# DeltaNet and a maxout layer on one core: the opening's chain rebuilt, and identity products put into TensorE's waits

## The chip, the cores and the metric

One core of one Trainium2 chip. The metric is the time of one execution in microseconds (us), the median of three runs. The engines are named as the profile names them: PE (matrix products; PEld its weight loads), DVE (VectorE), ACT (ScalarE), POOL (GpSimd), SP (SyncE, which here only issues DMAs). Each works through its own instructions in order and waits on semaphores for the others.

## The reference

Attention of the delta-rule kind, then a feed-forward layer with the maximum of three products:

```python
B, H, S, D = 4, 8, 768, 48
k_n = k / (np.linalg.norm(k, axis=-1, keepdims=True) + 1e-06)
state = np.zeros((B, H, D, D))
for t in range(S):
    kt, vt, bt = k_n[:, :, t], v[:, :, t], beta[:, :, t, None]
    y[:, :, t] = einsum('bhd,bhde->bhe', q[:, :, t], state)
    v_old = einsum('bhde,bhd->bhe', state, kt)
    state = state + bt[..., None] * einsum('bhd,bhe->bhde', kt, vt - v_old)
x = y as (3072 tokens, 384)
h = max(x @ w1, x @ w2, x @ w3)      # 384 x 768 each
out = h @ w_out                      # 768 x 384
```

## The kernel before, in words

The recurrence is cut into 12 chunks of 64 positions. In each chunk the 64 updates depend on one another through a triangular system, one for each of the 32 (batch, head) pairs, made of the products of the keys among themselves, scaled by beta over the squared norms. The kernel inverts the 32x32 diagonal blocks of these systems by elimination on DVE (`solve`), for two chunks at a time, 128 blocks side by side on the partitions, and joins the blocks by small products on PE. With the inverse, the updates of a chunk are products, and the state is carried from chunk to chunk. Queries, keys and values come from DRAM; a token's outputs are turned (`to_x`) and go into the feed-forward layer, which runs over six groups of 512 tokens.

The order of all instructions is written out by hand, engine by engine (a manual schedule): the order of the Python calls is the order of each engine's queue. Nothing reorders it.

The opening is what comes before the first feed-forward product, the calls from `busy(6, ident)` to the loop over `ffn(0)`. Its steps, with the names that later text uses:

- `turn(n, (0,))` and `turn(n, (1,))` transpose the keys or queries of unit n on PE (a unit is one chunk of two of the four batches); ACT, once DVE, copies the result from PSUM (L335). `kpad`, `kmore` and `qall` are the loaded keys and queries.
- `keys(n)` and `gram(n, (1,))` are the key-by-key and query-by-key products (`p_g`, L406) with a copy from PSUM to `at` (L423) or `pt` (L417). For the units 4 to 7 the blocks go by DMA to DRAM (`to_dram`, L436, on SP) and come back block by block (`blocks(1)`, L483, issued on POOL).
- For the units 0 to 3 `to_blocks` (L467, L465) copies the blocks from `at` and `first_blocks` (L471) transposes them all in one DVE instruction.
- `solve(0)` computes the norms (`norm`, L261 to L266: a root on ACT and five small DVE instructions that refine it), the inverse, its square times beta (L523 to L525), writes the diagonal (L529), scales (L538), and runs 15 steps of two DVE instructions (L552, L556). It then transposes the solution (L564) and `placed` (L496) copies it, block by block, into `ut`. `solve(1)` does the same for the next two chunks in 31 steps, a few after each feed-forward group.
- `halves_t` (L633, L635) transposes the solution for the left side of a product. `halves_z` (`p_e`, L673) and `halves_u` (`p_f`, L684, L688) join 16x16 halves to 32x32 blocks, `turn_t1` (L618, L620), `join_z` (`p_z`, L701, L705) and `join_u` (`p_j`, L714, L716) join 32x32 blocks to 64x64.
- `new(0)` (`p_u`, L759, L764) gives the updates, `to_y(0)` (`p_y`, L801, L805) the outputs, `to_x(0)` (`p_x`, L820, L827) turns them. `masked` (L390) applies the triangle to `pt`. `scale` (L287) multiplies the values by the norms, which `first_norms` (L302) has transposed on DVE.

The weights arrive as 64-bit numbers. `fetch` loads one of 24 pieces (L215, on SP or POOL); one step of `conv` turns a piece into 32-bit numbers with three ACT instructions (L238 to L240), and `joined` (L250 on DVE, L254 on POOL) puts the halves of the piece before together.

PSUM is handed out in two rings: `two`, three buffers of two banks, and `ffn`, two buffers of one bank. A product waits until the buffer's earlier reader is done. `busy(n, of)` runs n products of the identity with itself into an `ffn` buffer that nobody reads; one such product is two passes of 128x128 over 128 columns. Before the change it is called once, at the start.

After the opening, `ffn(0)` yields after each group of products (`hidden`, L1161, L1169, L1175), and the loop puts the other work between the groups: `FIRST` lists the links of the first chunks (`e1`, `f1`, `z1`, `j1` are the joins of chunk 1, `s0` the state's step, `S1` one step of the solve, `M2` and `M3` masks of query products, `P4` the product itself with its mask), and `CONVERTED` the groups after which a weight piece is converted.

Of the kernel before, what the change touches and what calls it, by code (L numbers as in the profile page):

```python
# [16 lines left out]
C = 64  # L17
DP = 64
BL = 32
# [4 lines left out]
def kernel(  # L24
# [196 lines left out]
    def weights():  # L221
# [3 lines left out]
        waiting = None  # L225
        for dst, _, (a, b) in pieces:
# [14 lines left out]
            if waiting:  # L241
                joined(*waiting)
            waiting = dst, mant, mant_v, up_v
            yield
        joined(*waiting)
        yield

# [11 lines left out]
    def norm(out, ksum, root, t):  # L259

        nc.scalar.sqrt(root, ksum)  # L261
        nc.vector.tensor_scalar_max(t, root, 1e-30)
        nc.vector.reciprocal(t, t)
        nc.vector.tensor_tensor(out=t, in0=t, in1=ksum, op=ALU.mult)
        nc.vector.tensor_tensor(out=t, in0=t, in1=root, op=ALU.add)
        nc.vector.tensor_scalar(  # L266
            out=out, in0=t, scalar1=0.5, scalar2=1e-6, op0=ALU.mult, op1=ALU.add
        )

# [29 lines left out]
    bl_0 = []  # L299

    def first_norms():
        nc.vector.transpose(out=nrm_0.rearrange("p c g h -> p (c g h)"), in_=bl_0[0])  # L302
# [152 lines left out]
    def to_blocks(n, engines):  # L455


        cc, g = divmod(n, 2)
        for i, engine in enumerate(engines):
            bb, half = divmod(i, 2)  # L460
            r, x0 = block(bb, half), 16 * cc + 8 * g
            to = in_rows(in_wo(0))[r, x0 : x0 + H]
            of = ats[n][r, :, BL * half : BL * (half + 1)]
            if engine is nc.scalar:
                engine.copy(to, of)  # L465
            else:
                engine.tensor_copy(to, of)  # L467
# [21 lines left out]
    def placed(cc, i, copy=nc.vector.tensor_copy, xs_of=slice(0, 2 * H)):  # L489
# [6 lines left out]
        copy(to[:, xs_of], of[:, xs_of])  # L496

    def solve(m):
# [13 lines left out]
        bl = small("bl", BL)  # L512
        norm(bl, diagonal(x), small("root_bl", BL), small("nt_bl", BL))
# [3 lines left out]
        if m:  # L517
            norms_of(m, bl)
            nc.vector.reciprocal(bl, bl)
        else:  # L520
            bl_0.append(bl)
            bl = small("inv_bl", BL)
            nc.vector.reciprocal(bl, bl_0[0])  # L523
        nc.vector.tensor_tensor(out=bl, in0=bl, in1=bl, op=ALU.mult)
        nc.vector.tensor_tensor(out=bl, in0=bl, in1=beta_bl[:, m] if m else beta_0, op=ALU.mult)  # L525
# [12 lines left out]
        nc.vector.tensor_tensor(out=xb, in0=xb, in1=by, op=ALU.mult)  # L538
        yield
        for j in range(size - 1):  # L540
            a, b = j + 1, size - 1 - j
# [20 lines left out]
        if m == 0:  # L562
            back = in_rows(xs[0])
            nc.vector.transpose(out=back, in_=y.rearrange("p c i -> p i c"))  # L564
            yield
            for i in range(4):
                if i % 2:
                    n = H * (i == 3)
                    if n:
                        placed(0, i, nc.vector.tensor_copy, slice(0, n))  # L570
                    placed(0, i, nc.scalar.copy, slice(n, 2 * H))
                else:
                    placed(0, i, nc.vector.tensor_copy)
            return
# [52 lines left out]
    def halves_t(c, parts=(0, 1)):  # L627
        if c not in fine:
            fine[c] = [square("t") for g in range(2)]
        src = [ut[c % NU][:, g].rearrange("p h x -> p (h x)") for g in range(2)]  # L630
        dst = [t.rearrange("p h x -> p (h x)") for t in fine[c]]
        if 0 in parts:
            nc.vector.transpose(out=dst[0], in_=src[0])  # L633
# [30 lines left out]
    def halves_z(c):  # L664
        if c > 1:
            halves_t(c)
# [807 lines left out]
```

## Time and profile before

| | us |
|---|---|
| median of three runs | 513.03 |
| the runs | 512.97, 513.03, 517.85 |
| span of the profiled execution | 510.5 |
| what lies around the span, against the median | 2.5 |

The profiled execution's own time isn't listed apart from the runs; its span stands 2.5 us below the median, and that difference is used wherever spans and medians are compared.

| engine | busy us | share of the span |
|---|---|---|
| PE | 491.1 | 96% |
| PE weight loads | 333.1 | 65% |
| DVE | 349.9 | 69% |
| ACT | 168.7 | 33% |
| POOL | 192.7 | 38% |

The page cuts the span into 40 slices of 12.8 us, and gives for each the busy tenths of each engine and the clock that the throttle granted to PE (9 is 0.9 or more of full speed). Other views give the busy time of each engine in a chosen stretch, with the clock as a number, and the instructions in order of time: start, duration, engine, line, operation, what it writes and reads, shape, how many, and, in brackets, the idle time of the engine before it with what ended it. A matrix product with 32-bit operands counts as two passes, so 32 products show as x64; a transposition on PE is one pass.

### The profile page before, as it was taken

Reading aid. Unit: us, or ns where it says so; the run is one execution under the profiler, and the core shown is the slowest. Engines: PE = TensorE matmul, PEld = TensorE weight load, DVE = VectorE, ACT = ScalarE, POOL = GpSimd, SP = SyncE. Lnnn points to the kernel's source line nnn. Section 1 sums busy time; section 2 is a strip of 40 time slices with the busy share of each in tenths; the row PEclk is TensorE's granted clock in tenths of the full one; section 3 lists DMA queues with packets and bytes.
Section 4 is the critical chain, followed back from the end, with each engine's and each line's share of the span. In section 5 each row is a group of like instructions: output and inputs, shape, how many; then the busy total and the mean of one; then the engine's idle time right before and its main releaser. Section 6 shows DMA issues by size and latency. Waiting matters only on the chain.

```text
span 510.5 us, 18528 instructions
## 1 busy us (share of the span) xinstructions
PE 491.1 (96%) x8016; PEld 333.1 (65%) x8016; DVE 349.9 (69%) x801; ACT 168.7 (33%) x320; POOL 192.7 (38%) x317
## 2 busy tenths in 40 slices
PE   7778989999999999999999999999999999999996
PEld 6567778756565565665555565555655556998796
DVE  5897799969996430899563987635897455456752
ACT  5585664884422242210252101252101412113210
POOL 7434372783491926670575770503130000000000
PEclk9755999999999999999999999999999999999999
DMA  8938869764055925353675454923343202230001
GB/s 111 192 64 221 194 151 155 195 199 100 5 148 140 175 46 130 99 143 83 144 136 130 120 137 94 174 37 92 80 116 81 44 3 64 54 71 2 0 17 46
DMA packets 106304, 53.49 MB, mean 105 GB/s; under 512 B 89712, under 2 KB 99984, under 8 KB 106224
## 3 DMA queue, kind: packets, MB, share of 16 engines
q1 hardware_dynamic: 94352, 31.35, 30.4%
q0 software_dynamic: 9472, 20.37, 16.4%
q8 instruction: 63, 1.03, 0.9%
q10 hardware_dynamic: 2400, 0.59, 0.6%
q14 instruction: 17, 0.14, 0.1%
HBM read 39.17 MB, written 13.11 MB: 102 GB/s over the span
## 4 chain that ended last, share of the span: by engine, by line
PE 73%; DVE 14%; DMA 5%; ACT 4%; SPq 2%; issue 2%; POOL 0%; DVEq 0%; ACTq 0%; POOLq 0%
PE p_h L1161 26%; PE p_o L1199 13%; PE p_o L960 9%; PE p_e L1102 3%; DVE tmp L552 3%; PE p_g L406 3%; PE p_c L1102 2%; PE p_m L894 2%; PE p_u L759 2%; DMA kmore<-in_k_dram 2%; PE p_k L731 2%; PE p_y L801 2%; DVE y_bl L556 2%; PE p_s L782 2%; PE p_j L714 1%
## 5 line engine op out<-in xcount | busy, mean ns | idle before, releaser
L1161 PE MATMUL p_h<-xt,w_sb 128*128 128x512 f32 (+1 forms) x450 | 187.5, 558 | 0.7 <-ACT xt L827 0.6
L1161 PEld LDWEIGHTS p_h<-xt,w_sb 128*128 128x128 f32 x450 | 82.3, 193 | 68.7 <-issue 61.8
L1199 PE MATMUL p_o<-wo_sb,h 128*128 128x384 f32 x192 | 65.3, 490 | 0.0
L1175 DVE TENSOR_TENSOR h<-h,p_h 128x512 f32<-128x512 f32 (+1 forms) x42 | 25.4, 606 | 53.9 <-PE p_h L1161 52.8
L552 DVE TENSOR_TENSOR tmp<-x_bl,y_bl 128x31 f32<-128x31 f32 (+20 forms) x139 | 51.3, 369 | 4.1
L556 DVE TENSOR_TENSOR y_bl<-y_bl,tmp 128x31 f32<-128x31 f32 (+20 forms) x139 | 48.5, 349 | 4.8
L1199 PEld LDWEIGHTS p_o<-wo_sb,h 128*128 128x128 f32 x192 | 35.7, 190 | 23.2
L364 POOL DMA_DIRECT2D turned<-in_q_dram x72 | 39.1, 551 | 4.3 <-POOL turned L359 2.9
L1205 ACT COPY o_sb<-p_o 128x384 f32<-128x384 f32 x16 | 7.7, 479 | 85.8 <-PE p_o L1199 79.8
L1171 ACT ACTIVATE h<-p_h 128x512 f32<-128x512 f32 x24 | 14.3, 597 | 63.4 <-PE p_h L1161 60.5
L254 POOL TENSOR_TENSOR w_sb<-mant,up 128x384 int32<-128x384 int32 x18 | 19.1, 1059 | 39.3 <-DVE mant L250 39.2
L406 PEld LDWEIGHTS p_g<-kqt 48*64 48x64 f32 x1216 | 24.6, 142 | 9.0 <-issue 6.4
L406 PE MATMUL p_g<-kqt 48*64 48x64 f32 (+1 forms) x1216 | 27.8, 242 | 0.9 <-ACT kqt L335 0.8
L789 DVE TENSOR_TENSOR st<-st,p_s 48x768 f32<-48x768 f32 (+1 forms) x18 | 17.1, 949 | 15.4 <-PE p_s L782 15.2
L120 POOL DMA_DIRECT2D kpad<-in_k_dram x32 | 21.8, 690 | 14.1 <-issue 12.7
L1199 PE MATMUL p_o<-w_sb,xt 128*128 128x384 f32 x72 | 25.2, 486 | 0.0
L139 POOL DMA_DIRECT2D v_t<-in_v_dram x14 | 11.5, 829 | 35.5 <-PE p_u L759 35.5
L390 DVE TENSOR_TENSOR pt<-p_g,mask 128x512 f32<-128x512 f32 x20 | 13.8, 688 | 15.9 <-PE p_g L406 15.8
L287 POOL TENSOR_TENSOR v_t<-v_t,nrm 128x768 f32<-128x768 f32 x12 | 17.9, 1493 | 9.0 <-DVE nrm L281 8.9
L359 POOL MEMSET turned<- 128x96 f32 x18 | 3.3, 192 | 47.6 <-DVE kqt L380 47.6
L759 PEld LDWEIGHTS p_u<-v_t,ut 64*64 64x64 f32 x768 | 13.4, 141 | 10.1 <-issue 7.8
L1199 PEld LDWEIGHTS p_o<-w_sb,xt 128*128 128x128 f32 x72 | 13.7, 190 | 9.5
(212 smaller groups left out, 837.0 us busy)
## 6 DMA issues: line engine op xcount, KB each, us to landing
out_dram<-o_sb SPq DMA_DIRECT2D x40, 96.0 KB
w_bits<-in_moe_w_dram SPq DMA_DIRECT2D x9, 384.0 KB
w_bits<-in_moe_w_dram POOLq DMA_DIRECT2D x9, 384.0 KB, 5.2
turned<-in_q_dram POOLq DMA_DIRECT2D x72, 48.0 KB, 2.9
kpad<-in_k_dram POOLq DMA_DIRECT2D x32, 96.0 KB, 6.1
y_x<-y SPq DMA_DIRECT2D x16, 192.0 KB
qall<-y_x SPq DMA_DIRECT2D x32, 96.0 KB
v_t<-in_v_dram POOLq DMA_DIRECT2D x14, 192.0 KB, 5.0
```

What stands on the lines that cost most here:

```text
L120: queues[bb].dma_start(out=dst[rows(bb ^ g), :, 0:D], in_=src[2 * bb + g, :, c * C : (c + 1) * C, :].rearrange("h p d -> p h d"),)
L254: nc.gpsimd.tensor_tensor(out=dst.bitcast(I32), in0=mant_v.bitcast(I32), in1=up_v, op=ALU.add)
L364: (queue, nc.gpsimd)[i].dma_start(out=t[p0 : p0 + 32, bb, at : at + NP * 2 * D].rearrange("p (j x) -> p j x", j=NP), in_=(k, q)[i][2 * bb ...
L406: nc.tensor.matmul(p_g[rows(bb ^ (g * i)), par, c0 : c0 + C * (1 + whole)], kq[:, 0], kq if whole else kq[:, i],)
L552: nc.vector.tensor_tensor(out=t_v, in0=row.to_broadcast(t_v.shape), in1=column.to_broadcast(t_v.shape), op=ALU.mult,)
L556: nc.vector.tensor_tensor(out=rest, in0=rest, in1=t_v, op=ALU.subtract)
L759: nc.tensor.matmul(p_v[rows(bb ^ g), g, i], ut[c % NU][rows(bb), g, h], rhs[rows(bb), g, h],)
L960: nc.tensor.matmul(to[:, g], a[j][:, 128 * g : 128 * (g + 1)], b[j], start=(start and g == j == 0), stop=(stop and g == 1 and j == PAIRS - 1),
L1102: nc.tensor.matmul(to, w[stays], moves, start=(n == 0), stop=(n == len(terms) - 1))
L1161: nc.tensor.matmul(p_h, w_sb[i][:, t, f * 128 : (f + 1) * 128], xt[:, t, lo : lo + w], start=(t == 0), stop=(t == KT - 1),)
L1175: nc.vector.tensor_tensor(out=h, in0=h, in1=p_h, op=ALU.max)
L1199: nc.tensor.matmul(p_o, stays, moves, start=(n == 0), stop=(n == len(terms) - 1))
```

## The change

The diff has two kinds of edits. The first rebuild the opening's order and its operations:

- the norms: `norm` becomes `inverse_squares` (one root on ACT, one DVE sum, one DVE reciprocal), which is what the solve needs, and `norms`, which has a second root on ACT and four POOL operations; the norms' transposition in later solves moves behind the solve's first step, and in the first it becomes a PE product (`first_norms`);
- the blocks of the units 0 to 3 are copied straight from PSUM (`first_keys`);
- the solution of `solve(0)` is transposed in halves (`turn_back`), the upper columns first, and placed in halves; the transposed left sides are made of one transposition (`turn_half`) and eight small copies on three engines (`halves_t`), into tiles that POOL has zeroed (`zero_halves`);
- copies of `halves_z` go to ACT alone, `join_z` of chunk 0 fills all partitions so that two copies replace four, one copy of `to_x(0)` goes to DVE;
- the fourth unit's query transposition moves behind `to_x(0)` and its product into the feed-forward part (`P3` in place of `M3`); `solve(1)` starts after `to_x(0)`; the third weight fetch moves behind `keys(7)`; one weight conversion moves from the opening to the seventh group, and `join_first` puts a converted piece together at named places.

The second put 23 more identity products into the opening in twelve places (`busy`).

```diff
+    EPS = 1e-6
+    def inverse_squares(out, square_of, ksum):
+        nc.scalar.activation(out=square_of, in_=ksum, func=...Sqrt, scale=4.0 * EPS * EPS)
+        nc.vector.scalar_tensor_tensor(
+            out=square_of, in0=square_of, scalar=EPS * EPS, in1=ksum, op0=ALU.add, op1=ALU.add)
+        nc.vector.reciprocal(out, square_of)
+    def norms(out, square_of, inverse, t):
+        mult = nc.gpsimd.tensor_tensor
+        nc.scalar.sqrt(out, square_of)
+        mult(out=t, in0=out, in1=out, op=ALU.mult)
+        mult(out=t, in0=t, in1=inverse, op=ALU.mult)
+        nc.gpsimd.tensor_scalar(out=t, in0=t, scalar1=-0.5, scalar2=1.5, ...)
+        mult(out=out, in0=out, in1=t, op=ALU.mult)
...
     def first_norms():
-        nc.vector.transpose(out=nrm_0.rearrange("p c g h -> p (c g h)"), in_=bl_0[0])
+        p_n = ps_ffn([128, TOK], "p_n")[:, 0:BL]
+        for bb in range(2):
+            for f in range(2):
+                r = block(bb, f)
+                nc.tensor.matmul(p_n[r], bl_of[0][r], ident[r, r])
+        nc.scalar.copy(nrm_0.rearrange("p c g h -> p (c g h)"), p_n)
...
+    def turn_back(s):
+        cols = slice(HB * s, HB * (s + 1))
+        nc.vector.transpose(
+            out=in_rows(xs[0])[:, cols], in_=ys[0].rearrange("p c i -> p i c")[:, cols])
+    def turn_half():
+        nc.vector.transpose(
+            out=first_half().rearrange("p c x -> p (c x)"),
+            in_=ys[0][:, 0:HB].rearrange("p c i -> p (c i)"))
+    def halves_t(c, engines):
+        for n, engine in enumerate(engines):
+            f, bb, g = n // 4, n // 2 % 2, n % 2
+            ...
+            copy(fine[c][g][block(bb ^ g, f), :, BL * f : BL * f + HB],
+                 first_half()[block(bb, f), :, x0 : x0 + H].rearrange("p c h -> p h c"))
...
     turn(0, (0,))
     turn(1, (0,), nc.vector.tensor_copy)
-    keys(0, None)
-    to_blocks(0, (P, P, P, P))
+    first_keys(0, (V, V, P, P), nc.scalar.copy)
     turn(2, (0,))
-    keys(1, None, nc.vector.tensor_copy)
-    to_blocks(1, (V, V, V, P))
+    first_keys(1, (V, V, V, P), nc.scalar.copy)
     turn(3, (0,))
-    keys(2, None)
-    ...
+    later = [first_keys(2, (A, V, A, V)), first_keys(3, (V, A, V, V))]
     first_blocks()
+    for whole in later:
+        whole(nc.scalar.copy)
     load_q(2, (nc.gpsimd, nc.gpsimd))
     turn(4, (0,))
+    some(solving, 1)
     turn(5, (0,))
-    some(solving, 1)
     keys(4)
     keys(5)
     turn(6, (0,))
+    busy(4, ident)
     turn(0, (1,))
+    busy(1, ident)
...
+    zero_halves(0)
+    zero_halves(1)
     keys(6)
+    busy(1, ident)
     gram(0, (1,), None, later=True)
     turn(7, (0,))
+    busy(1, ident)
     turn(1, (1,))
     keys(7)
+    busy(1, ident)
+    fetch(nc.sync)
     turn(2, (1,))
+    first_norms()
     gram(1, (1,), None, later=True)
-    turn(3, (1,))
     some(conv, 1)
     gram(2, (1,), None, later=True)
-    gram(3, (1,), None, later=True)
-    some(solving, HB + 1)
-    halves_t(0)
+    busy(6, ident)
+    scale(0, nrm_0[:, 0])
+    some(solving, HB)
+    turn_back(1)
+    for i in range(4):
+        placed(0, i, A.copy if i % 2 else V.tensor_copy, high)
+    turn_half()
+    halves_t(0, (V, V, P, P, V, P, V, A))
     halves_z(0)
-    ...
+    busy(1, ident)
+    turn_back(0)
+    for i in (1, 3, 0, 2):
+        placed(0, i, V.tensor_copy if i % 2 else P.tensor_copy, low)
+    halves_u(0)
+    turn_t1(0)
+    busy(2, ident)
+    join_z(0)
+    busy(2, ident)
+    masked(pts[0], by_par(pts[0]))
+    masked(pts[1], by_par(pts[1]))
+    join_first()
     blocks(1, nc.gpsimd)
     ...
     join_u(0)
+    placed(1, 0)
+    placed(1, 1, nc.gpsimd.tensor_copy)
     old_k(0)
     old_q(0)
+    busy(1, ident)
     new(0)
-    some(conv, 1)
     fetch(nc.gpsimd)
     load_v(1, nc.gpsimd)
+    placed(1, 2)
+    to_y(0)
     placed(1, 3)
-    to_y(0)
-    halves_t(1)
+    halves_t(1, (V, V, P, P, V, V, P, P))
+    busy(2, ident)
+    to_x(0)
+    busy(1, ident)
+    some(conv, 1)
+    join_first()
+    turn(3, (1,))
     solving = solve(1)
     some(solving, 1)
-    to_x(0)
     some(conv, 1)
...
-        3: "j1 S1 q1 M3 S1 S1", ...
+        3: "j1 S1 q1 P3 S1 S1", ...
-    CONVERTED = {*range(6), *range(11, 25)}
+    CONVERTED = {*range(7), *range(11, 25)}
```

## The prediction

> **What bounds the kernel now.** I read the page first: engine shares, the 40 slices, the chain that ended last.
>
> ```profile
> span 510.5 us, 18528 instructions
> PE   7778989999999999999999999999999999999996
> PEclk9755999999999999999999999999999999999999
> PE 73%; DVE 14%; DMA 5%; ACT 4%; SPq 2%; issue 2%; POOL 0%; DVEq 0%; ACTq 0%; POOLq 0%
> ```
>
> From the fifth slice on TensorE (PE) is full and at full clock, so what the opening loses is lost for good, and what it gains stays if later stages don't take it back. Only the first four slices (51 us) show waits and a low clock. The span is 510.5 us; the runs' median is 513.03, so 2.5 us lie around the span, and I forecast in the median's terms.
>
> Next, busy time in stretches cut where the granted clock changes. They are 3.41 us apart, or multiples of it. Columns: stretch, length, PE, PE weight loads, DVE, ACT, POOL, clock, DMA share, GB/s.
>
> ```profile
> 12.06:15.48 3.42, 1.77 (x68) 1.46 (x68) 2.85 (x6) 2.07 (x6) 2.19 (x3) 1.00 0.98 169
> 15.48:18.89 3.41, 2.75 (x68) 2.45 (x68) 2.76 (x12) 1.56 (x3) 1.98 (x4) 0.50 0.97 148
> 18.89:22.30 3.41, 3.41 (x53) 2.74 (x46) 3.03 (x12) 1.94 (x5) 2.23 (x4) 0.50 1.08 255
> 22.30:25.72 3.42, 1.96 (x56) 1.51 (x59) 3.04 (x12) 1.80 (x4) 0.00 (x0) 1.00 1.33 185
> 32.54:35.96 3.42, 3.04 (x124) 2.69 (x117) 2.71 (x9) 3.03 (x10) 2.65 (x2) 0.50 0.22 35
> 46.20:49.61 3.41, 3.41 (x91) 2.70 (x93) 2.67 (x8) 0.73 (x2) 0.37 (x1) 0.50 0.89 194
> 49.61:53.02 3.41, 3.41 (x57) 2.96 (x50) 1.93 (x6) 1.78 (x4) 2.82 (x3) 0.50 0.80 170
> 53.02:56.44 3.42, 3.42 (x135) 2.92 (x135) 1.28 (x3) 1.77 (x5) 1.74 (x2) 1.00 0.83 207
> ```
>
> The clock is half from 15.5 to 22.3 and from 25.7 to 53.0. Busy time doesn't decide it: 46.20 to 49.61 is 100% busy and half speed follows. I weighed each product by columns moved times the share of the 128x128 array its tile covers (a pass of 128x128 over 128 columns is 128; one of a 64x64 tile over 32 columns is 8). Per stretch that gives 1536, 1536, 1792, 1536 for the first four, 500 for 32.54, 1312 for 46.20, 1760 for 49.61. Full clock followed the stretches of 1760 and more; half clock followed those of 1536 and less. One later stretch speaks against a sharp line: 63.26 to 66.68 holds 1408 (up to 1660 with a product that began before it) and stayed full.
>
> Last, instructions in order of time, for the chain from the first keys to the first feed-forward product.
>
> ```profile
> 12.20 1.98 DVE L471 STREAM_TRANSPOSE x_bl<-wo_sb 128x1024 f32<-128x1024 f32 x1
> 14.51 0.18 DVE L262 TENSOR_SCALAR nt_bl<-root_bl 128x32 f32<-128x32 f32 x1 [0.32 <-ACT root_bl L261]
> ...
> 26.30 1.98 DVE L564 STREAM_TRANSPOSE x_bl<-y_bl 128x1024 f32<-128x1024 f32 x1
> 28.31 1.58 DVE L496 COPY ut<-x_bl 32x512 f32<-32x512 f32 x3
> ...
> 29.62 2.45 PE L673 MATMUL p_e<-ut,at 64*64 64x32 f32 x63 [2.30 <-ACT ut L496]
> ...
> 44.39 2.93 PE L1161 MATMUL p_h<-xt,w_sb 128*128 128x256 f32 x6 [0.57 <-ACT xt L827]
> ```
>
> PE stands 2.30 us before p_e: the opening is a DVE chain (blocks 12.20, root 14.21, solve 17.64 to 26.26, transposition, copies), then small products between ACT and DVE copies, at half clock, to 44.39. Then two feed-forward groups at half clock, until p_f starts at 53.40.
>
> **Part 1, to the start of the solve.** Blocks from PSUM: eight DVE copies after 8.5, at 0.42 each (nearest row, a PSUM copy of 128x256 on DVE), end at 11.9. They replace two DVE copies of 0.69 and five of 0.40, and POOL's last copy at 11.91. Gain 0.3 (bounds -0.3 and 0.8). Root: eight small DVE instructions become three. Gone are 0.18 + 0.22 + 0.19 + 0.18 + 0.35 + 0.19, new is one of 0.22, and five gaps of 0.03 go: gain 1.25. The POOL copy (0.69) stays. The second root and four POOL operations on 128x32 run beside the solve. So the solve starts at 16.1; its 8.62 us are untouched; it ends at 24.7.
>
> The cost: ACT now has both roots before the copy of the fifth key transpose, which waits to 14.75 instead of 12.4, and the next key product behind it on PE waits to 15.4. The stretch to 15.48 then holds only some 800, so the clock drops there as before. I count nothing: DVE is the bound until 24.7, and a four-fold identity product stands there to raise it.
>
> **Part 2, solve to first feed-forward product**, counted from the solve's end. Half transposition 1.0 (half of 1.98), ACT's two copies 0.95 (0.45 each; 32x256 took 0.40), so p_e may start at +2.0; before it started at +3.4. On PE, the fourth query transpose and product leave (0.6 + 0.9, and a wait of 1.46 for their DMA), and 14 identity products (28 passes) come in before p_e: 3.9 at 0.14 a pass warm (their weight load takes 0.14), 6.8 cold (0.244: the start's 12 passes in 2.93). Summing PE's queue from the late key product on, with the other products at their warm rows, it ends near 27.3 instead of 26.7 when p_e's data are there: I add 0.6 (bounds 0 and 1.5). From p_e on, with PE at full clock (p_e 1.1, p_f 1.1, p_z 0.75, p_j 0.75, p_u 1.1, p_y 1.1, p_x 0.96, from the same lines at 53 to 75):
> z copies end +3.5; the second half's DVE copies (four of 0.22) +3.3; p_f +3.4 to 4.5; ACT's six negations of 0.27 to 0.29 end +5.75; p_z to +6.15; z copies, now two instead of four, +6.6; DVE's three transpositions (1.35) end +7.0; p_j to +7.75; masks 2 x 0.69, one mantissa shift 0.35 and the negation 0.42 on DVE end +9.2; p_u +9.75; p_y +10.95; DVE's y copy +11.5; p_x +12.5; a placed copy (0.6) and four small copies hold DVE to +13.0, its xt copy ends +13.5. First p_h at 24.7 + 13.55 + 0.6 = 38.9: 5.5 earlier.
>
> **Part 3, the next two groups.** From 44.39 to 53.40 is 9.0 us with PE full at half clock. At full clock PE needs 1.4 + 1.1 + 1.1 + 1.4 = 5.0. ACT is then last: two conversions (1.6 each), the moved query transpose's copy 0.59, two roots 0.27, the zero fill 1.03, h copy 0.37, z copy 0.59, from 37.9 to 44.1. So p_f starts at 44.2: 9.2 earlier.
>
> **Part 4, given back.** The fourth query product moves to the fourth group: PE 0.69 there, its ACT copy of 0.59 gone, its DVE mask equal. One weight conversion moves to the seventh group (DVE 0.35, POOL 1.0, ACT 1.7), where DVE is 95% busy. The norms of later solves are read by DVE one step late from POOL's four operations: 0.10 (a memset) to 0.69 (the strided copy) each, so 0.4 to 2.8 a solve, against four DVE instructions (0.8) saved. I take 0. Queues: the third weight fetch leaves SP's place before the 16 key writes, where it held SP for 3.21 us, so these writes start earlier. The read of these blocks stands on POOL behind a weight sum that waits for DVE's shift: issue at about 35, landing 39 (3.6 us), wanted by ACT at 40. Given back: 1.2.
>
> **Sum:** 5.5 + 3.7 - 1.2 = 8.0. 513.0 - 8.0 = **505.0** (span 502.5).
>
> **A rule against it.** Row first: from 29.62 to 44.39 PE has no wait over 0.8 us, yet the clock stays half. The Trainium skill, "TensorE: Matmul & The Clock Gate", section "Why this matters for your kernels", asks only for no PE gap over about 3 us between bursts. By it the clock would have been full there already and unread products would buy nothing: the sum would be part 1 and the copies of part 2, some 4 us. The measured clock decides against it.
>
> **Rivals.** (a) *The clock falls once more on the way.* Around p_z and p_j my count in 3.4 us is p_z 256, identity products 512 and 256, p_j 128, some 150 of p_u: 1300; with the stretches where they lay before it is about 1600 and 1700. Against 1536 and 1760 that is open. If it falls there, p_u, p_y, p_x and the first groups run at half: 3 to 4 us back, 508.5. (b) *Unread products don't move the clock at all*, and it stays half until dense feed-forward products raise it: only parts 1 and 2's shorter chain stay, 4 - 1.2: 510. (c) *Slower.* The identity products stand in order on PE before real ones. 46 passes at 0.244 are 11.2 us; the waits of PE between 12.06 and 44.39 sum to 8.1, of which the shorter chain takes some 4. If the clock stays half and fewer waits than about 7 us are where the products stand, the opening becomes PE-bound: 11.2 less 4 filled, less 1.2 of real products moved out: 6 later, 519. The start's row (2.93 for six products) speaks for the price; against it, dense 128x128 work like this raised the clock at 22.3 and 53.0.
>
> **Chances:** forecast 0.55, (a) 0.25, (b) 0.13, (c) 0.07. The forecast's own range is 502 to 507.5. The range reaches into (b) and, below, to a chain with no backlog and a shorter second solve: 501.5 to 511.5. Within 1% (5.1 us) is about what a measurement here can tell from no change: faster by over that 0.62 (the forecast and part of (a)), same 0.32, slower 0.06.
>
> **What would show it.** Clock 1.00 from about 25 on without a break; p_e at about 27, p_h at 39, p_f at 44; the solve's first step at 16. PE waits before p_j and p_u on DVE, ACT full from 38 to 44. Wrong if the clock is 0.50 anywhere past 27, if DVE waits for POOL at the norm transpositions, or if ACT waits for weight DMAs.

## The result, and the profile after

| | before | after |
|---|---|---|
| median, us | 513.49 | 547.78 |
| lowest to highest, us | 512.97 to 517.85 | 546.05 to 548.21 (4 runs) |
| the profiled execution: its time, its span, us | not listed apart; 510.5 | 548.21; 546.3 |

The ratio is 1.064, with a 95% interval of 1.059 to 1.070. The changed kernel is 34 us slower, where 8 us faster was forecast. In the profiled execution of after 1.9 us lie around the span (548.21 less 546.3); the 2.5 used for before compares different executions. The page of the changed kernel, its span, PE's busy tenths and clock in 40 slices, and the shares of the chain that ended last:

```profile
span 546.3 us, 18654 instructions
...
PE   6888789999999999489999639999999999999996
...
PEclk9678879999999999879999959999999999999999
...
PE 81%; DMA 5%; POOL 5%; issue 4%; DVE 3%; ACT 2%; SPq 0%; POOLq 0%; DVEq 0%
```

Before, PE's row was full from the fifth slice on. Now it has two holes, at slices 17 and 23 to 24 (from 218 and from 300 us), each with a low clock, and POOL, which had no share in the chain, has 5%. These holes have nothing to do with the opening. I took the starts of the same feed-forward products in both traces, 978 in each. The difference, after less before (products counted from 0):

| product | before at | after later by |
|---|---|---|
| first p_h | 44.39 | 4.65 |
| 12th | 55.41 | 1.9 |
| 24th | 62.26 | 7.8 |
| from the 30th to the 276th | 66.8 to 213 | 8.2 to 10.2, at the end 9.5 |
| 288th | 219.09 | 20.3 |
| 432nd | 291.68 | 36.5 |
| from there to the end | | 35.8 |

So 27.0 us come in two jumps, 10.8 and 16.2, in `solve(3)` and `solve(4)` (the opening's is `solve(0)`); some 8 to 9 come before 75 us. The first hole, as busy time in stretches (columns: stretch, length, PE, PE weight loads, DVE, ACT, POOL, clock, DMA share, GB/s), after:

```profile
220.00:225.00 5.00, 5.00 (x136) 3.02 (x134) 0.19 (x1) 1.40 (x2) 4.35 (x10) 1.00 0.49 141
225.00:230.00 5.00, 0.32 (x1) 0.00 (x0) 0.00 (x0) 0.00 (x0) 4.73 (x11) 0.88 0.59 159
230.00:235.00 5.00, 1.12 (x43) 1.15 (x45) 4.62 (x14) 0.00 (x0) 4.20 (x6) 0.50 0.20 49
```

For five microseconds only POOL works. What it does, in order of time, and who waits, on DVE and on PE (after):

```profile
219.77 3.81 POOL L386 DMA_DIRECT2D kmore<-in_k_dram  x7 [1.77 <-issue]
...
224.06 0.55 POOL L386 DMA_DIRECT2D kmore<-in_q_dram  x1 [0.29 <-POOL kmore L381]
224.96 3.81 POOL L386 DMA_DIRECT2D kmore<-in_q_dram  x7 [0.35 <-DMA kmore<-in_k_dram]
228.79 0.25 POOL L281 TENSOR_TENSOR root_bl<-bl 128x32 f32<-128x32 f32 x1
...
229.76 0.25 POOL L286 TENSOR_TENSOR bl<-bl,root_bl 128x32 f32<-128x32 f32 x1
```

```profile
230.04 0.88 DVE L299 STREAM_TRANSPOSE nrm<-bl 64x32 f32<-64x32 f32 x4 [9.85 <-POOL bl L286]
...
232.84 0.95 DVE L796 TENSOR_TENSOR v_t<-v_t,p_k 128x768 f32<-128x768 f32 x1
```

```profile
233.88 1.96 PE L812 MATMUL p_u<-v_t,ut 64*64 64x48 f32 x64 [8.56 <-issue]
```

The four operations of the norms take 1.2 us, but they stand on POOL behind 15 DMA issues of key and query blocks at 0.55 us each, some of which wait in turn for an earlier transfer. DVE stands at the norms' transposition for 9.85 us; behind it in DVE's queue is the subtraction into `v_t` (L796), which p_u needs. The clock falls, and p_u and the feed-forward products behind it run at half from 228.81 to 239.06. The second hole is the same with 14.75 us on DVE and half clock from 314.15 to 327.8:

```profile
318.66 0.88 DVE L299 STREAM_TRANSPOSE nrm<-bl 64x32 f32<-64x32 f32 x4 [14.75 <-POOL bl L286]
```

In the trace of before the norms were five DVE instructions, and the transposition there had no wait:

```profile
208.75 0.18 DVE L266 TENSOR_SCALAR bl<-nt_bl 128x32 f32<-128x32 f32 x1
208.97 0.88 DVE L281 STREAM_TRANSPOSE nrm<-bl 64x32 f32<-64x32 f32 x4
```

Now the opening, in the order in which the prediction took it: the blocks, the transposition, the solve's first step, p_e and the first p_h, after (the same steps before: 12.20, 17.64, 29.62, 44.39):

```profile
11.96 0.87 DVE L506 COPY wo_sb<-p_g 32x256 f32<-32x256 f32 x2 [0.43 <-ACT wo_sb L506]
13.27 0.87 DVE L506 COPY wo_sb<-p_g 32x256 f32<-32x256 f32 x2 [0.43 <-ACT wo_sb L506]
14.24 1.96 DVE L511 STREAM_TRANSPOSE x_bl<-wo_sb 128x1024 f32<-128x1024 f32 x1
...
18.24 0.19 DVE L601 TENSOR_TENSOR tmp<-x_bl,y_bl 128x30 f32<-128x30 f32 x1
```

```profile
11.57 0.36 ACT L506 COPY wo_sb<-p_g 32x256 f32<-32x256 f32 x1 [0.69 <-DVE wo_sb L506]
12.87 0.36 ACT L506 COPY wo_sb<-p_g 32x256 f32<-32x256 f32 x1 [0.94 <-DVE wo_sb L506]
...
30.14 0.62 ACT L239 ACTIVATE up<-w_bits 128x384 f16<-128x384 f32 x1
...
31.21 1.29 ACT L545 COPY ut<-x_bl 32x256 f32<-32x256 f32 x2
```

```profile
29.12 1.60 PE L1283 MATMUL p_w<-ident 128*128 128x128 f32 x12
31.88 0.30 PE L724 MATMUL p_e<-ut,at 64*64 64x32 f32 x4 [1.16 <-ACT ut L545]
...
36.90 1.93 PE L756 MATMUL p_z<-ut,at 32*64 32x32 f32 x64
...
49.04 1.53 PE L1214 MATMUL p_h<-xt,w_sb 128*128 128x256 f32 x6 [1.62 <-ACT kqt L357]
```

ACT and DVE read the same PSUM tile in turn, and each stands waiting for the other's semaphore. The solve starts later than before, not earlier. ACT reaches its placed copies 3.1 us after DVE's transposition has ended (28.08), because a query product's copies and a weight conversion stand ahead of them. And the clock, by the same columns as above:

```profile
30.85:34.26 3.41, 2.01 (x82) 1.74 (x83) 2.94 (x6) 2.76 (x6) 2.02 (x4) 1.00 0.48 134
34.26:37.67 3.41, 3.41 (x97) 3.12 (x92) 1.66 (x5) 1.61 (x6) 0.16 (x1) 0.50 0.04 10
37.67:41.09 3.42, 3.42 (x113) 3.07 (x110) 1.82 (x5) 1.19 (x4) 1.41 (x2) 0.50 0.01 2
41.09:44.49 3.40, 3.40 (x106) 3.18 (x110) 1.99 (x4) 1.15 (x3) 3.35 (x5) 0.50 0.68 227
```

The stretch with p_e's wait (59% busy) cost the clock, and then PE is full with products and identity products for 10.2 us at half speed.

How much of such times belongs to the kernel and how much to the one execution that was profiled can be seen in runs that have the same instructions up to there. p_e started at 29.62, 31.52 and 29.49 in before and the two runs below that change only its later solves; at 31.88, 30.35 and 31.29 in after, with the norms by DVE, and with the norms read late; at 32.20 and 29.62 in the two runs without identity products that differ in the later solves alone. So up to 2.6 us of a time in one profile's opening can be the execution's.

### The profile page after: what moved, and what is told of

The parts are those of the page before. It is cut to its first block, busy times and chain, and to the rows that moved or that the text cites. A ratio compares the mean times of both kernels' runs of the same rounds, so it can differ in the third digit from the quotient of the medians.

```text
span 546.3 us, 18654 instructions
## 1 busy us (share of the span) xinstructions
PE 503.2 (92%) x8070; PEld 342.4 (63%) x8070; DVE 344.0 (63%) x778; ACT 169.5 (31%) x327; POOL 204.5 (37%) x349
## 3 DMA queue, kind: packets, MB, share of 16 engines
q0 software_dynamic: 9472, 20.37, 14.8%
## 4 chain that ended last, share of the span: by engine, by line
PE 81%; DMA 5%; POOL 5%; issue 4%; DVE 3%; ACT 2%; SPq 0%; POOLq 0%; DVEq 0%
PE p_h L1214 28%; PE p_o L1252 16%; PE p_o L1013 8%; PE p_g L428 4%; PE p_u L812 3%; PE p_e L1155 3%; PE p_c L1155 2%; POOL kmore L386 2%; DMA turned<-in_k_dram 2%; PE p_y L854 2%; PE p_t L351 2%; PE p_j L767 2%; PE p_k L784 2%; PE p_z L756 2%; PE p_s L835 2%
## 5 line engine op out<-in xcount | busy, mean ns | idle before, releaser
L1252 PE MATMUL p_o<-wo_sb,h 128*128 128x384 f32 x192 | 68.5, 508 | 0.0
L1228 DVE TENSOR_TENSOR h<-h,p_h 128x512 f32<-128x512 f32 (+1 forms) x42 | 25.5, 608 | 54.2 <-PE p_h L1214 53.7
L1252 PEld LDWEIGHTS p_o<-wo_sb,h 128*128 128x128 f32 x192 | 37.2, 199 | 24.8 <-issue 2.9
L812 PE MATMUL p_u<-v_t,ut 64*64 64x48 f32 x768 | 17.5, 249 | 22.2 <-issue 22.2
L812 PEld LDWEIGHTS p_u<-v_t,ut 64*64 64x64 f32 x768 | 15.8, 163 | 30.2 <-issue 30.2
L428 PEld LDWEIGHTS p_g<-kqt 48*64 48x64 f32 x1088 | 22.0, 139 | 11.8 <-issue 7.9
L428 PE MATMUL p_g<-kqt 48*64 48x64 f32 (+1 forms) x1088 | 25.0, 240 | 4.0 <-issue 2.2
L842 DVE TENSOR_TENSOR st<-st,p_s 48x768 f32<-48x768 f32 (+1 forms) x18 | 17.1, 950 | 15.0 <-PE p_s L835 14.7
L139 POOL DMA_DIRECT2D v_t<-in_v_dram x14 | 11.6, 832 | 35.7 <-PE p_u L812 35.7
L817 ACT COPY u<-p_u 128x768 f32<-128x768 f32 (+1 forms) x12 | 9.3, 771 | 45.2 <-PE p_u L812 45.2
```

Source lines behind the costliest of these rows:

```text
L428: nc.tensor.matmul(p_g[rows(bb ^ (g * i)), par, c0 : c0 + C * (1 + whole)], kq[:, 0], kq if whole else kq[:, i],)
L812: nc.tensor.matmul(p_v[rows(bb ^ g), g, i], ut[c % NU][rows(bb), g, h], rhs[rows(bb), g, h],)
L1228: nc.vector.tensor_tensor(out=h, in0=h, in1=p_h, op=ALU.max)
L1252: nc.tensor.matmul(p_o, stays, moves, start=(n == 0), stop=(n == len(terms) - 1))
```

## The experiments

All ratios are to the kernel before, run beside each on the same chip, with 95% intervals. Theory and rivals carry the letters of the texts on record.

| run | median us | ratio | interval |
|---|---|---|---|
| after: norms by DVE | 520.5 | 1.012 | 1.008 to 1.016 |
| after: norms read late | 520.7 | 1.012 | 1.007 to 1.017 |
| before: norms by POOL | 540.4 | 1.051 | 1.046 to 1.057 |
| after: no identity products | 539.6 | 1.049 | 1.044 to 1.055 |
| read late, no identity products | 516.4 | 1.006 | 1.003 to 1.009 |
| read late, conversion put back | 527.4 | 1.027 | 1.021 to 1.034 |
| read late, one engine a tile | 522.6 | 1.017 | 1.010 to 1.025 |
| before: identity products | 516.7 | 1.007 | 1.003 to 1.011 |
| before: new root, read late | 517.9 | 1.006 | 1.003 to 1.008 |
| read late, no products, conversion behind | 518.1 | 1.007 | 1.004 to 1.010 |
| the same, one engine a tile | 516.7 | 1.005 | 1.001 to 1.008 |
| norms by DVE, no products, one engine a tile | 512.0 | 0.998 | 0.994 to 1.002 |

**Norms by DVE.** The changed kernel, with the four operations of the solves 1 to 5 on DVE.

```diff
-    def norms(out, square_of, inverse, t):
-        mult = nc.gpsimd.tensor_tensor
+    def norms(out, square_of, inverse, t, engine=nc.gpsimd):
+        mult = engine.tensor_tensor
...
-        norms(norm_bl, square_bl, inverse, small("root_bl", BL))
+        norms(norm_bl, square_bl, inverse, small("root_bl", BL),
+              nc.vector if m else nc.gpsimd)
```

> The changed kernel, with the four small operations of the norms on DVE instead of POOL in the solves 1 to 5; all else as changed. Theory Q (POOL's queue): in the fourth and fifth solve these operations stand on POOL behind 32 to 48 DMA issues of 0.55 us, and DVE's norm transposition waits for them; that gives 10.8 + 16.2 us. So this kernel is near 548 - 27 = 521, the two jumps against the kernel before (at its 219 and 286 us) are gone, and DVE's waits for POOL at the norm transposition (25.6 us) too. Rival O (the opening): what the opening does to the clock and to the order of loads comes back later as these stalls; then the jumps stay and the time is 540 or more.

Both jumps are gone, and DVE's transposition has no wait:

```profile
221.06 0.88 DVE L299 STREAM_TRANSPOSE nrm<-bl 64x32 f32<-64x32 f32 x4
```

The run is 9.6 us behind the kernel before at the 276th product, and 9.4 behind it after both solves. The gain, 547.8 less 520.5, is 27.3.

**Norms read late.** The operations stay on POOL; only DVE's transposition moves, in the solves 3 to 5, from behind the first step to behind the twelfth.

```diff
-            if m and j == 1:
+            if m and j == (12 if m > 2 else 1):
                 norms_of(m, norm_bl)
```

> The changed kernel, norms still on POOL, but in the solves 3 to 5 DVE transposes them before step 12 instead of before step 1. Theory Q: only the early read costs, so this is within 2 us of the run with the norms on DVE, some 521 to 523. Rival P (POOL's operations themselves: they wait for ACT and DVE and hold up the DMA issues behind them, whoever reads them): the jumps stay, 538 or more.

Here POOL does all it did in the changed kernel, and the time is the same as with DVE's norms, 520.7. The same stretches in this trace:

```profile
220.00:225.00 5.00, 5.00 (x76) 2.97 (x75) 3.88 (x11) 0.80 (x1) 4.23 (x9) 1.00 0.64 164
225.00:230.00 5.00, 5.00 (x140) 3.34 (x138) 2.20 (x6) 0.48 (x1) 1.21 (x4) 1.00 0.13 30
```

So the 27 us aren't POOL's work, nor the POOL operations' delay of the loads behind them, but come from the place of one DVE instruction in DVE's queue.

**The kernel before with POOL's norms.** The other way about: only this edit, in the old kernel (solves 1 to 5).

```diff
+        if m:
+            inverse_squares(bl, square_bl, diagonal(x))
...
+        if m:
+            norms(norm_bl, square_bl, inverse, small("root_bl", BL))
...
+            if m and j == 1:
+                norms_of(m, norm_bl)
```

> The kernel before, with the new norms in the solves 1 to 5 alone (one root for the solve, four POOL operations, the transposition before step 1); opening and identity products as before. Theory Q: this one edit carries the two jumps, 513 + 27 = 540, between 533 and 545. Rival O: without the changed opening there are no jumps, 511 to 515.

The old opening gets both jumps, 10 and 15.1 us, and nothing else (0.16 at the last product before the first). DVE's rows at the norms in this trace:

```profile
220.91 0.88 DVE L306 STREAM_TRANSPOSE nrm<-bl 64x32 f32<-64x32 f32 x4 [10.06 <-POOL bl L293]
```

This settles 27 of the 34 us, from both sides. It leaves some 7 to the rest of the change.

**Without the identity products.** The changed kernel without the 23; and the same with the norms read late.

```diff
-    busy(4, ident)
     turn(0, (1,))
-    busy(1, ident)
...  (all twelve places)
```

> The changed kernel without the 23 added identity products. Both theories on the later jumps leave them here. For the opening: if the products cost more (PE's queue runs late before p_e) than their clock saves, the first feed-forward product comes earlier than 49.0 and the time is 2 to 4 us below 548; if they save, it comes later and the time is 1 to 4 us above.

> Norms read late (as in the run before with them) and none of the 23 added identity products. Theory N (the products themselves cost about 8 us, as 547.8 against 539.6 said): 520.7 - 8 = 512.5, the opening reaches the first feed-forward product near 48 and the clock doesn't fall again behind it. Rival M (the 8 us are only where the clock's steps happened to lie in that run): 518 to 522.

Without them the changed kernel is 8.2 us faster, and with the norms read late 4.4 us faster (520.7 less 516.4; by the ratios 3 us, with intervals that just overlap). The second lies between what theory N (512.5) and rival M (518 to 522) gave. They are not a neutral filling: they cost more than the clock that they hold.

**Identity products alone.** The kernel before with the 23 products in the answering places.

```diff
+    busy(6, ident)
     some(solving, HB + 1)
     halves_t(0)
     halves_z(0)
+    busy(1, ident)
...
```

> The kernel before with the 23 identity products at the places that answer to those of the change, nothing else. Theory N: they cost there too, 515 to 520 (46 passes at 0.14 to 0.24 are 6 to 11 us of PE time, of which the waits between 12 and 44 us hide a part). The prediction's own idea (they hold the clock and save): 508 to 511, with the clock full from 26 on. Rival M: 512 to 515.

PE in order of time, in this run:

```profile
27.92 2.46 PE L1230 MATMUL p_w<-ident 128*128 128x128 f32 x12
30.34 0.31 PE L673 MATMUL p_e<-ut,at 64*64 64x32 f32 x6
...
34.69 1.04 PE L701 MATMUL p_z<-ut,at 32*32 32x32 f32 x64 [0.37 <-ACT ut L688]
...
45.46 2.21 PE L1161 MATMUL p_h<-xt,w_sb 128*128 128x256 f32 x6
```

They do move the clock: it is full from 29.75 to 43.40, where before it was half. Yet the first p_h starts 1.07 later than before: from p_e to it there are 15.1 us, mostly at full clock, against 14.8 at half. Apart from one on p_y (1.48 us at 42.14, for nothing that the profile shows) the waits there end on ACT and DVE, so the copies and not PE's speed seem to set this path. Later the clock falls once more (67.29 to 70.71), and the run ends 3.4 us behind.

**The conversion put back.** Norms read late, and the weight conversion that the change took out of the opening back in it.

```diff
     new(0)
+    some(conv, 1)
...
-    CONVERTED = {*range(7), *range(11, 25)}
+    CONVERTED = {*range(6), *range(11, 25)}
```

> Norms read late, products kept, and one weight conversion back in the opening (before the updates' product), so that a piece is joined one group earlier, as in the kernel before. Theory W (weights one group late): PE's wait for POOL's weight sum before the fourth group (1.5 to 2.1 us) and the half clock behind it go: 516 to 518. Rival N (the products' place in the opening): no change beyond 1 us from 520.7, the loss stays between the first and the fifth group.

It is 7 us slower than the run that it is made from, not faster. The idle times on PE, in order of time:

```profile
53.70 0.68 PE L835 MATMUL p_s<-u,kpad 64*64 64x48 f32 x14 [1.46 <-issue]
61.90 0.88 PE L784 MATMUL p_k<-st,kqt 48*64 48x48 f32 x20 [2.88 <-issue]
...
91.91 2.72 PE L1214 MATMUL p_h<-xt,w_sb 128*128 128x256 f32 x6 [2.44 <-DVE y_p L605]
```

One of them is a late DVE; two have no cause in the profile, and about each of these the clock falls to half (53.7 to 57.1, 60.6 to 67.4). PE's waits for `w_sb` are gone in this trace (2.05 us before the fourth group in after, 0.54 and 1.45 in the run that it is made from), so theory W had the cause of that wait; but the time doesn't come back with it.

**One engine for each tile.** Norms read late; the blocks of unit 2 copied by ACT alone, of unit 3 by DVE alone.

```diff
-    later = [first_keys(2, (A, V, A, V)), first_keys(3, (V, A, V, V))]
+    later = [first_keys(2, (A, A, A, A)), first_keys(3, (V, V, V, V))]
```

> Norms read late, products kept, and of the blocks copied from PSUM each of the last two tiles is read by one engine alone (unit 2 by ACT, unit 3 by DVE). Theory S (ACT's and DVE's reads of one PSUM tile wait for each other): the waits between them go, the blocks' transposition starts near 12.6 instead of 14.2, the first solve step near 16.7, and the time is 1 to 1.5 us below 520.7. Rival: the waits aren't what sets this time (the last key product is): the transposition starts at 13.8 or later.

The waits between the two engines are gone, as DVE's rows show:

```profile
11.00 1.72 DVE L506 COPY wo_sb<-p_g 32x256 f32<-32x256 f32 x4 [0.19 <-PE p_g L485]
12.86 1.93 DVE L511 STREAM_TRANSPOSE x_bl<-wo_sb 128x1024 f32<-128x1024 f32 x1
```

The transposition starts 1.0 us earlier than in the run that it is made from (13.85 there), and so do the solve and the first p_h (47.51 against 48.50). The total doesn't show it (522.6 against 520.7, the intervals overlap).

**The new root without the new opening.** The kernel before with POOL's norms in the solves 1 to 5, read late (the diff is against the run with POOL's norms in the kernel before). As the diff has it, the transposition stands behind the solve's first step in the solves 1 and 2 and behind the twelfth in 3 to 5, one step earlier than the text on record counts.

```diff
-            if m and j == 1:
+            if m and j == (12 if m > 2 else 1):
                 norms_of(m, norm_bl)
```

> The kernel before, with the new form of the root in solves 1 to 5 (three instructions on DVE fewer ahead of the first step, norms by four operations on POOL), and the norms' transposition put behind the solve's second step (solves 1 and 2) or its thirteenth (solves 3 to 5), so that DVE doesn't stand in wait for POOL. The opening is that of the kernel before. Theory Q (the order of DVE's queue alone made the 27 us): neither jump, 511 to 514.5 us, between 2 us faster than the kernel before and 1 us slower; the root that is 1.25 us shorter in five solves gives at most 6 us if every solve is on the path, and the trace of before has PE at its full clock behind those solves, so little. Rival R (POOL's four operations delay the block loads behind them, and these the next solve): one jump stays, of 3 us or more, 517 us or above.

No jump, but neither the 0 that theory Q gave: 3 us slower. To 327 us it runs level (-0.2); then it loses 1.2, 1.7 and 0.5 in the solves 4 and 5. New waits of PE stand there that before hasn't:

```profile
390.24 2.81 PE L1195 MATMUL p_h<-xt,w_sb 128*128 128x512 f32 x6 [1.52 <-DVE xt L895]
...
404.69 0.72 PE L735 MATMUL p_z<-ut,at 32*32 32x32 f32 x60 [0.83 <-DMA ut<-y_d]
```

Reading the norms late has a price of its own: from 294 us to the last product all seven runs that read late lose 1.0 to 3.3 us against before, while after and the five others lie between -0.8 and +0.4, POOL's norms among them. The run also bounds what the rebuilt opening is worth: the run without identity products and this one differ in the opening and what moved with it, both with the norms read late, and stand at 1.006 both, with intervals that leave some 2 us either way open.

**The conversion behind p_e.** Without the identity products, norms read late; the opening's first weight conversion behind p_e on ACT. Then the same with one engine for each tile.

```diff
     gram(1, (1,), None, later=True)
-    some(conv, 1)
     gram(2, (1,), None, later=True)
...
     halves_z(0)
+    some(conv, 1)
     turn_back(0)
```

> The changed kernel with norms read late and without the identity products, and with the opening's first piece of the weight conversion moved from ahead of the solve's remaining steps to behind the first query product p_e, so that on ACT its 1.6 us no longer stands ahead of the copies that p_e waits for. Theory X (ACT's queue is what kept p_e back by 3 to 4 us): p_e starts near 29, three microseconds earlier than without the move, and the first feed-forward product near 44.5 instead of 46.7; total 513 to 515 us. Rival Y (the weights come late instead, or the clock's phase swallows it): total 515.5 to 519 us, with waits for the weights in the first groups of the feed-forward.

> As the run before it, and with the blocks of queries 2 and 3 each copied from PSUM by one engine (ACT the third, DVE the fourth) instead of both engines in turn. Theory S (the two engines serialise on one PSUM tile): the blocks' transposition starts 1 us earlier, the solve too; total 511.5 to 514.5 us if that microsecond lasts, equal within 1 us to the run before it if the clock swallows it.

Neither is told from the run without the move (516.4). In the first, ACT did stand free, 3.73 us ahead of its placed copies, but they waited for DVE:

```profile
25.56 2.53 DVE L601 TENSOR_TENSOR tmp<-x_bl,y_bl 128x78 f32<-128x78 f32 x1
28.12 0.24 DVE L605 TENSOR_TENSOR y_bl<-y_bl,tmp 128x78 f32<-128x78 f32 x1
```

One DVE instruction of 0.24 us took 2.53. It ends 0.11 us after an operation of POOL, the multiplication of the values by the norms (`scale`):

```profile
26.49 1.49 POOL L305 TENSOR_TENSOR v_t<-v_t,nrm 128x768 f32<-128x768 f32 x1
```

The run that this one is made from lost 1.5 us to such an instruction in the same place (1.72 for 0.22), and there too ACT's copies waited for DVE. Without the identity products ACT's queue isn't the bound, so theory X isn't borne out by these two. In after, with the products, the rows above show ACT's queue last before p_e.

**The opening alone.** What is left of the change when norms are done by DVE, the identity products are gone and each tile has one reader: the chain and the root.

```diff
+              nc.vector if m else nc.gpsimd)
...
-    busy(4, ident)
...
+    later = [first_keys(2, (A, A, A, A)), first_keys(3, (V, V, V, V))]
```

> The changed kernel with the norms of solves 1 to 5 by DVE (no wait for POOL, and no norms that come late), without the 23 identity products, and with the blocks of queries 2 and 3 each copied by one engine: what is left of the change is the opening's chain (blocks from PSUM, one root, solution transposed in halves) and the shorter root. Theory Z (the rebuilt opening is worth nothing, since the two runs that differ in the opening alone, both with the norms read late, stand at the same ratio): 512 to 516 us. Rival F (the forecast's 3.7 us from p_h to p_f and 1 us from the undivided copies last to the end once the norms and the products are gone): 508 to 511 us. In both, the time from the first p_h to the first p_f is near 5.5 us.

512.0 us, ratio 0.998 with an interval from 0.994 to 1.002: no difference that this measurement can tell. It is the best of the variants, but not shown to be faster than the kernel before. Its solve, too, holds a DVE instruction of 1.51 us instead of 0.19. Its first p_f starts at 50.71, 2.7 us earlier than before; by the 24th feed-forward product it is 0.9 later. What it gained went here (stretches of this run and then of before):

```profile
53.00:58.00 5.00, 3.38 (x74) 2.60 (x75) 4.73 (x13) 3.16 (x7) 2.05 (x3) 0.98 0.99 230
58.00:65.00 7.00, 7.00 (x169) 5.77 (x168) 4.02 (x12) 5.35 (x10) 0.99 (x1) 0.53 0.89 177
```

```profile
53.00:58.00 5.00, 5.00 (x202) 4.10 (x202) 2.69 (x9) 3.31 (x8) 1.74 (x2) 1.00 0.81 213
58.00:65.00 7.00, 5.93 (x187) 4.54 (x185) 6.70 (x18) 6.04 (x12) 1.98 (x2) 1.00 0.77 174
```

PE arrives early and finds the weights not ready. Its waits from 53 to 58 are for `w_sb` on POOL (0.58 and 0.48) and one of 0.76 with no cause shown; by 57.77 the clock falls, and stays half until 64.60.

## Why the prediction was wrong, step by step

**The step that failed** is in part 4: "The norms of later solves are read by DVE one step late from POOL's four operations: 0.10 (a memset) to 0.69 (the strided copy) each, so 0.4 to 2.8 a solve ... I take 0." It measured 27.0 us, 10.8 in `solve(3)` and 16.2 in `solve(4)`. The four operations took 0.21 to 0.25 us each, inside my bounds; the price was never theirs. I bounded a wait by the duration of the work waited for, and didn't look at what stands ahead of that work on POOL. The trace of before had it: at the same places POOL issues blocks of DMAs (its busy time is 4.30 of the 5 us from 215 to 220). It even had the price. There the transposition ended at 209.85, and POOL came to `scale`, which needs it, 9.65 us later, when its DMA issues were through:

```profile
219.50 1.49 POOL L287 TENSOR_TENSOR v_t<-v_t,nrm 128x768 f32<-128x768 f32 x1
```

An operation put on POOL at that place comes out of the same queue. For the weight conversion I did name POOL's queue; for this edit I didn't. The text named "DVE waits for POOL at the norm transpositions" among what would make it wrong, and gave it no place in the range and no part in a rival.

**Part 1** gave the solve's first step at 16.1; it came at 18.24, 0.6 later than before. The root's part is right: from the end of the transposition to the first step it is 2.04 us against 3.46, a gain of 1.4 where 1.25 was forecast. The blocks' part is wrong: I counted the copies from PSUM one after the other on DVE and left out that ACT reads the same tile. Undividing them brought 1.0 back and left the transposition at 12.86, still 0.7 behind the 12.20 of before.

**Part 2** gave the first p_h at 38.9; it came at 49.04. Of the 10.1, the late solve is 2.3 (its end 26.97 against 24.7). From there to p_e it is 2.3 more, on ACT and PE, where a conversion, the late query products and the 12 passes stood; part of that is the execution's, since p_e came 1.5 earlier in the run with norms by DVE, which has the same instructions up to it. From p_e to p_h it is 17.2 against 11.6: 5.6 more, mostly rival (a)'s mechanism, the clock falling before p_z, with 10.2 us of full PE at half speed, which is up to 5.1 more than at full speed, where I priced 3 to 4 (the 5.1 is an estimate that takes half the clock for twice the time).

**Part 3** was right: from first p_h to p_f 5.6 us, against 5.3 forecast and 9.0 before. But this gain didn't last. I stopped the sum at p_f and took for granted that PE stays full from there; in all variants it then waited for weights or fell to half clock between 57 and 75 us, and the run with the opening alone lost there what it had gained.

**The identity products**: rival (c) had their place and direction. With the norms repaired the changed kernel stands at 520.5, near its 519, but without them (norms read late) it is only 4.4 us faster, so they are a part of that, not all; that 519 was nearly met is partly luck. In the old kernel they cost 3.4 us (1.0066 of 513) although the clock was full for 13.65 us in a row: a full clock on products that wait for copies buys little. Rival (b), that they don't move the clock, fell with that run.

**The count of columns times array share**, on which the forecast of the clock rested, fell. In after a stretch of 1792 with 0.34 us of waits (17.19 to 20.61) was followed by half clock, and one of 1376 without a wait (41.09 to 44.49) by full. In the kernel before 1312 without a wait gave half. A stretch without a wait and of some 1376 would fit these, but in the run without identity products one with 0.29 us of waits (45.49 to 48.90) was followed by full as well; a rule it isn't. The Trainium skill's rule that I weighed against the change ("TensorE: Matmul & The Clock Gate", section "Why this matters for your kernels": no PE gap over about 3 us between bursts) doesn't hold here either: waits of 1.16 and 0.37 us in the stretch from 30.85 to 34.26 were enough to lose the clock. The same table asks, for reaching the full clock, that TensorE be busy for 4 us or more continuously, which my text left out; here three stretches in which PE was busy throughout (34.26 to 44.49) passed before it came back.

**The sum**, in the measured parts: the norms' wait +27; the identity products +4.4; reading the norms late and the rest +2.9, of which the traces show 1.0 to 3.3 behind 294 us in the runs that read late; the opening nothing that can be told from 0, or -1.1 (-3.1 to +0.9) with its copies undivided and the norms by DVE. Of the forecast's 8.0 nothing is left that can be measured.

## What to carry to other kernels

When an operation moves to another engine, its price is what stands ahead of it in that engine's queue at that place, and on the reader's engine everything that stands behind the read. On an engine that issues DMAs, read the queue in order of time at each place where the operation will run, in late stages too. A gain in the opening is worth something only if what comes next (here the weights) is ready earlier as well. And before a difference of a few microseconds between two profiles is explained, look how far runs with the same instructions up to there differ: here by up to 2.6 us.

## What was not expected of the hardware

- **Idle PE with no cause in the profile**, 0.4 to 2.9 us, at the same few places of its instruction stream in different kernels: counted in weight loads and products before it, about 1703, 1955, 2210, 2463 and 2717, some 254 apart. Before, it was 1.27 us at 64.66; after, 2.25 at 67.49; the run with the conversion put back had 2.88. In each case a 16 KB packet of the queue of instructions had landed 1.2 to 1.9 us before PE went on. That fits a wait for its own instructions, but this wasn't tested.
- **Single DVE instructions of 1.2 to 2.5 us** instead of 0.2 to 0.4: one at the end of the first solve in each of the five runs of the changed kernel without identity products (1.72, 1.72, 2.53, 1.46 and 1.51). In four with them (norms by DVE, and the three others with the norms read late) the pair of placed copies right behind that solve took 1.62 to 2.10 instead of 0.80; before and after have none in that place. In all nine the long instruction ends 0.06 to 0.26 us after POOL's `scale` (L305, 1.5 to 1.7 us), which runs beside it; a DVE instruction that reads PSUM took its usual time beside it (L842: 0.95), and so did a transposition (L675 in after: 0.71). The changed opening puts `scale` ahead of the solve's last steps, where before had it behind them, at 34.46. That DVE stands still there for POOL fits all nine, but no run moved `scale`, so it isn't tested. It lies on the opening's path, at 0.8 to 2.3 us a run.
- **Two engines reading one PSUM tile** took turns, with 0.43 us of waiting on DVE and 0.69 to 0.94 on ACT at each change. Each wait ends on a semaphore of the other engine, so the program as built asks for the turns; what the chip would do without them no run here shows.
- **The clock's steps** are multiples of 3.41 us apart in every run, but the first one stood at 5.24 in before, 6.95 in after and 6.57 in the opening alone. The Trainium skill, "TensorE: Matmul & The Clock Gate", section "What's actually happening", says that the window is free-running and doesn't reset when a kernel starts; these rows agree. In two runs the clock rose for the first time at 25 us: the run without identity products, and the one with the conversion behind p_e and one engine a tile. The views write 1.00 for the time before the first step, so it has to be read from the products. These are four transpositions in the run without identity products, and then the same four in the run that also reads the norms late, where the clock rose at 5.45:

```profile
8.34 1.11 PE L351 MATMUL p_t<-ident,kpad 128*128 128x128 f32 x4
```

```profile
8.56 0.66 PE L351 MATMUL p_t<-ident,kpad 128*128 128x128 f32 x4
```

These two have the same instructions in the opening. So the clock's course there isn't the kernel's alone, a gain of a microsecond may turn into 3.4 us won or lost, and differences of up to 2.6 us between single profiles of these openings settle nothing.
